# Attention of the last three batches computed token-major, with the square sums from ScalarE's accumulator

## The chip, the cores and the metric

The kernel runs on one core of a Trainium2 chip. The metric is the device time of one execution in microseconds (us). A core has TensorE (matrix products, PE), VectorE (DVE), ScalarE (ACT), GpSimd (POOL, which here issues most loads) and SyncE (SP, which here issues stores and transposing DMAs). Each engine works through its own queue in order; semaphores join the queues.

## What is computed

```python
def _attn_ref(q, k, v, g_norm):                   # q, k, v: [8 batches, 8 heads, 576 tokens, 64]
    kv = np.einsum('bhsd,bhse->bhde', k, v)
    out = np.einsum('bhsd,bhde->bhse', q, kv)
    rms = np.sqrt(np.mean(out * out, axis=-1, keepdims=True) + 1e-06)
    return (out / rms * g_norm).astype(np.float32)

def _moe_ref(x, w_a, w_b, w_out):                 # x: [4608, 512], w_a, w_b: [512, 1536]
    a = x @ w_a
    b = x @ w_b
    return (a * b @ w_out).astype(np.float32)
```

The attention's result is laid out as x, one row for a token and 8 heads of 64 columns, and goes through the bilinear layer. So each token's 64 values of a head are divided by their root mean square and multiplied by `g_norm`.

## The kernel before

**Stages.** The 4,608 tokens are cut into nine blocks of 512. For each block the layer's first half multiplies x with w_a and w_b, combines the two results and gives `ab`; the second half multiplies `ab` with w_out one block later, so that the two halves are interleaved in TensorE's queue. All blocks but the first use a fast scheme with seven products in place of eight (`wino_block`, `o_block`): sums of blocks of x are made first (`t_op`, L711), the products (L742) accumulate in banks of PSUM, ScalarE copies what stands in a bank between two products of a chain (L415), and VectorE adds such a copy to another bank (L761) and multiplies the two halves (L796). The second half's products are L911, ScalarE's copies from them L943, VectorE's sums L949, its sums of `ab` L896, and the stores L814.

**Attention.** Batches 0 and 1 are loaded in another layout at the start. Batches 2 to 7 go through `load_node` and `late_batch`. For a batch, GpSimd issues a copy of q to a DRAM scratch `scr` (L566) and the loads of k and v (L572 to L582); SyncE issues one transposing DMA that brings q from the scratch to the tile `qT`, with d on the partitions (L587). A one-element copy on GpSimd (`gate_t`, L563) holds the next batch's load back until the transpose of the batch before has landed. TensorE then makes k times v for all heads (L533, 20 products of 128 columns) and ScalarE copies it to a block-diagonal tile `kvd` that holds two heads (L548, L549).

`slices` does the rest, in eight slices a batch: four pairs of heads times two halves of 288 tokens. In each slice x stands d-major, with 2 x 64 values of d on the partitions and tokens along the columns. So a sum over d runs over partitions, and TensorE makes it with a matrix of ones:

```python
n1: PE   x_mm   L348   kvd x qT           -> PSUM, 288 columns
n2: ACT  sq_op  L358   Square             -> sq, 128 x 288
n3: PE   s_mm   L362   ones x sq          -> PSUM, 288 columns
n4: ACT  rs_op  L366   Abs_reciprocal_sqrt -> rs, 128 x 288
    DVE  xt_op  L371   x * g_col * rs     -> xp, d-major, as the layer reads it
```

The tiles `xp` hold x of four batches in a ring.

**The order.** No loop order decides what runs when. Every piece is a node of `Plan`, with an engine, a duration from a small formula (`mm_us`, `act_us`, `dve_us`), a priority time, what it depends on and what buffers it takes. `Plan.order` goes through the nodes by simulated time and writes one order for every engine; what the chip then does is this order, with real waits. `Buf` and `Ring` hand out buffers: attention has a pool of three PSUM banks (`PA`), of which `RQ` and `RS` use two each. `at_win[b]` is the window of time over which a batch's attention is spread by priority.

Of the kernel before, what the change touches and what calls it, by code (L numbers as in the profile page):

```python
# [8 lines left out]
FP32 = mybir.dt.float32  # L9
BF16 = mybir.dt.bfloat16  # L10
FP16 = mybir.dt.float16
AF = mybir.ActivationFunctionType
# [123 lines left out]
def kernel(  # L136
# [11 lines left out]
    nc = tc.nc  # L148

    B, H, S, D = q.shape  # L150
    d_model = H * D
# [4 lines left out]
    NP = H // 2  # L156
# [25 lines left out]
    EH = d_model // 2  # L182

    const = ctx.enter_context(tc.tile_pool(name="const", bufs=1))
    scr_pool = ctx.enter_context(tc.tile_pool(name="scr", bufs=B, space=bass.MemoryType.DRAM))
    psum = ctx.enter_context(tc.tile_pool(name="psum", bufs=1, space=bass.MemoryType.PSUM))
    ctx.enter_context(tc.manual_schedule())

    def sb(name, shape, dt):
        return const.tile(shape, dt, name=name)  # L190
# [15 lines left out]
    as_t = sb("as", [128, 4, NJ, 256], FP16)  # L206
    b_ts = [sb(f"c{i}", [128, 4, 2, NMAX], FP16) for i in range(2)]
    u_t = sb("u", [128, 6, 2, NMAX], FP32)
    sq_ts = [sb(f"sq{i}", [128, HF], BF16) for i in range(3)]
    rs_ts = [sb(f"rs{i}", [128, HF], FP32) for i in range(3)]  # L210
    o_ts = [sb(f"o_sb{i}", [128, 4, d_model], FP32) for i in range(2)]

# [95 lines left out]
    def xcols(p, t0, n):  # L308
        return xp[p // 2][:, p % 2, t0 % R : t0 % R + n]
# [94 lines left out]
    def act_us(n, bias=False):  # L404
        return (0.155 if bias else 0.06) + n / 1200

    def dve_us(n):
        return (n + 65) / 960
# [7 lines left out]
        ]  # L416

    T0 = 20.0
    plan = Plan({"PE": 5.7, "DVE": 3.3, "ACT": 2.7, "SP": 5.0, "POOL": 22.5, "V": 0.0})
    PB, PA, PO = Pool(banks[0:4]), Pool(banks[5:8]), Pool(banks[4:5])  # L420
    RX, RY, RO = Ring(PB, 2), Ring(PB, 2), Ring(PO)
    RQ, RS = Ring(PA, 2), Ring(PA, 2)
    RU, RB, RAB = Ring([u_t[:, i] for i in range(6)]), Ring(b_ts), Ring(ab_ts)
    RT, RAS = Ring([T_t[:, i] for i in range(5)]), Ring([as_t[:, i] for i in range(4)])
    RSQ, RRS, ROS = Ring(sq_ts), Ring(rs_ts), Ring(o_ts)
    RK, RV, RQT, RKD = Ring(k_ts), Ring(v_ts), Ring(qT_ts), Ring(kvd)
    normed = {}
# [14 lines left out]
    def slices(at, win, extra):  # L442
        w0, w1 = win
        for i in range(2 * NP):
            p, h = divmod(i, 2)
            pr = w0 + (w1 - w0) * i / (2 * NP)
            x, s = ((Buf(RX), Buf(RY)) if at.b == 0 and i % 3 == 1 else (Buf(RQ), Buf(RS)))
            sq, rs = Buf(RSQ), Buf(RRS)
            ta = at.b * S + h * HF
            war = [  # L450
                n
                for j, (a, b) in enumerate(blocks_of)
                if a < ta - R + HF and b > ta - R
                for n in readers.get(j, ())
            ]
            n1 = plan.add(
                "PE", mm_us(1, HF), pr,
                lambda p=p, h=h, x=x: at.x_mm(p, h, x.tile), extra(p), [x], at.qt,
            )
            n2 = plan.add(  # L460
                "ACT", act_us(HF), pr, lambda p=p, h=h, b=sq: at.sq_op(p, h, b.tile), [n1], [sq]
            )
            n3 = plan.add(
                "PE", mm_us(1, HF), pr,
                lambda p=p, h=h, s=s: at.s_mm(p, h, s.tile), [n2], [s], [sq],
            )
            s_done[at.b] = n3
            n4 = plan.add(
                "ACT", act_us(HF, True), pr,
                lambda p=p, h=h, b=rs: at.rs_op(p, h, b.tile), [n3], [rs], [s],  # L470
            )
            normed[at.b, p, h] = plan.add(
                "DVE", dve_us(HF) + 0.06, pr,
                lambda p=p, h=h: at.xt_op(p, h), [n4] + war + ([g_n] if at.b == 0 else []), (), [x, rs],
            )

    def early_batch(b, win):
# [35 lines left out]
            done[p] = [n2, n4]  # L513
        slices(at, win, lambda p: done[p])

    def late_batch(b, load, win):
        at = Attn(b)
        w0, w1 = win
        kb, vb, qb = load["k"], load["v"], load["q"]
        kd = Buf(RKD)  # L520
        at.qt = [qb, kd]

        def view(t):
            return t[:, 0 : H * (NCH + 1) * D].rearrange("p (h c d) -> p h c d", h=H, d=D)

        s = Buf(RS)

        def kv_mm():
            kv_ps = s.tile[:].rearrange("p (a e) -> p a e", a=NP)
            for c in range(NCH + 1):  # L530
                for p in range(NP):
                    hs = slice(2 * p, 2 * p + 2)
                    nc.tensor.matmul(  # L533
                        kv_ps[:, p, :],
                        lhsT=kb.tile[:, c, hs, :],
                        rhs=view(vb.tile)[:, hs, c, :],
                        start=(c == 0 and p == 0),
                        stop=(c == NCH and p == NP - 1),
                    )

        n = plan.add(
            "PE", 1.15, w0, kv_mm, [(load["n"], load["kv_us"]), plan.at(w0 - 3)], [s, kd], [kb, vb]
        )

        def kv_out():
            kv_ps = s.tile[:].rearrange("p (a e) -> p a e", a=NP)
            at.kvd = kd.tile
            nc.scalar.copy(at.kvd[0:D, :, 0:D], kv_ps[0:D, :, 0:D])  # L548
            nc.scalar.copy(at.kvd[D:, :, D:], kv_ps[D:, :, D:])  # L549
            for p in range(NP):  # L550
                at.q[p] = qb.tile[:, p, :]

        m = plan.add("ACT", 0.75, w0, kv_out, [n], (), [s])
        slices(at, (w0 + 0.12 * (w1 - w0), w1), lambda p: [m, (load["qn"], 8.0)])


    def load_node(b, prio, dep):
        ld = {"k": Buf(RK), "v": Buf(RV), "q": Buf(RQT)}
        scr = scr_pool.tile([NP, S, 2, D], BF16, name="scr", tag="scr")

        def issue():
            if dep is not None:
                nc.gpsimd.tensor_copy(gate_t, dep["q"].tile[0:1, 0, 0:1])  # L563
            qv = q[b].rearrange("(p hl) s d -> hl s p d", hl=2)
            for hl in range(2):
                nc.gpsimd.dma_start(  # L566
                    out=scr[:, :, hl, :].rearrange("p s d -> s p d"), in_=qv[hl]
                )
            kt = ld["k"].tile
            ks = k[b, :, 0:SA, :].rearrange("h (sp c) d -> sp h c d", c=NCH)  # L570
            for c in range(NCH):
                nc.gpsimd.dma_start(out=kt[:, c], in_=ks[:, :, c, :])  # L572
            nc.gpsimd.dma_start(out=kt[0:SB, NCH], in_=k[b, :, SA:S, :].rearrange("h sp d -> sp h d"))
            for n, src in (("v", v),):
                t = ld[n].tile[:, 0 : H * (NCH + 1) * D].rearrange(
                    "p (h c d) -> p h c d", h=H, d=D
                )
                nc.gpsimd.dma_start(
                    out=t[:, :, 0:NCH, :],
                    in_=src[b, :, 0:SA, :].rearrange("h (sp c) d -> sp h c d", c=NCH),  # L580
                )
                nc.gpsimd.dma_start(  # L582
                    out=t[0:SB, :, NCH, :], in_=src[b, :, SA:S, :].rearrange("h sp d -> sp h d")
                )

        def transpose():
            nc.sync.dma_start_transpose(  # L587
                out=ld["q"].tile[:].rearrange("p a s -> p (a s)"),
                in_=scr[:].rearrange("a s h d -> (a s) (h d)"),
            )  # L590

        issue_us, q_us, ld["kv_us"] = (15.4, 4.3, 13.0) if dep is None else (9.0, 5.0 if b == 3 else 1.8, 13.0)

        ld["n"] = plan.add(
            "POOL", issue_us, prio, issue, [(dep["qn"], 8.0)] if dep else [], [ld["k"], ld["v"]]
        )
        ld["qn"] = plan.add(
            "SP", 2.5, prio, transpose, [(ld["n"], q_us)], [ld["q"]]
        )
        return ld  # L600
# [422 lines left out]
    for b in range(2, B):  # L1023
        t = b * S / N0
        at_win[b] = (max(53.0, st[int(t) - 1] + (t % 1) * L[int(t) - 1] - 18), st[int(t)] - 22 + (t % 1) * 12)
    loads = {2: load_node(2, 22.5, None)}
    wo_n = load_wo(loads[2])
    for b in range(3, B):
        loads[b] = load_node(b, at_win[b - 1][0], loads[b - 1])
    gb = Buf(RQ)  # L1030
    g_in = plan.add(
        "PE", 0.07, 8.5, lambda: nc.tensor.transpose(gb.tile[:, 0:1], g_row, one), [plan.at(6.4)], [gb]
# [10 lines left out]
    for bi in range(1, nb + 1):  # L1043
        o_win = (st[bi] + 1.0, st[bi + 1] - 1.0) if bi < nb else (st[bi] + O_A, st[bi + 1] + O_B)
        if bi == 1:
            o_std(ab, muls, (o_win[0] + 4.0, o_win[1] + 4.0))
            osum = out_sums(st[2] - 10)
        else:
            o_block(bi - 1, ab, muls, osum, o_win, 2, (RO, RY, RY), 1)
        for b in needs[bi]:  # L1050
            late_batch(b, loads[b], at_win[b])
        ab, muls = wino_block(bi, (st[bi], st[bi + 1]), wsum)
    o_block(
        nb, ab, muls, osum, (st[nb + 1], st[nb + 1] + o_us[nb]), NJ // 2,
# [38 lines left out]
```

## Time and profile before

| | |
|---|---|
| time, median of 3 runs | 299.74 us (299.61 to 299.81) |
| the profiled execution | 299.53 us |
| its span in the profile | 297.8 us |
| busy: PE, DVE, ACT | 290.5, 234.0, 192.4 us |
| the chain of waits, by engine | PE 71%, DMA 22%, POOL 4% |
| squares L358, roots L366, multiplies L371 | 64 each, 414, 508 and 511 ns |
| k times v (L533), first and last | 51.2 and 206.5 us |
| transposes of q (L587), first and last | 42.2 and 155.5 us |

The span is what the profile covers of the execution; the rest of its time lies around it. A group's row gives line, engine, operation, the tiles and shapes, the count, then busy time and mean length of one, then the time that the engine stood idle just before and what ended it. The chain of waits is followed back from the end of the execution: it is carried by DMA while the weights and first batches arrive, and from 79.5 us on by TensorE's products.

### The profile page before, as it was taken

What the parts mean: (1) busy time and instruction counts of PE and PEld (TensorE: products, weight loads), DVE (VectorE), ACT (ScalarE), POOL (GpSimd) and SP (SyncE); (2) the same over time, 40 slices, a digit from 0 to 9 for tenths busy, and PEclk for the clock granted to TensorE, in tenths of its full rate; (3) what the DMA queues carried; (4) which work ended last, traced back from release to release, by engine and by line L of the source; (5) the groups of instructions that cost most, each with busy time, mean ns of one, the idle gap of its engine ahead of it and who ended that gap; (6) DMA issues with size and microseconds to landing.
All of it is one profiled execution on the core that took longest, in us unless ns stands there. A gap on an engine that the chain in (4) does not pass through costs nothing.

```text
span 297.8 us, 6705 instructions
## 1 busy us (share of the span) xinstructions
PE 290.5 (98%) x2635; PEld 238.9 (80%) x2635; DVE 234.0 (79%) x435; ACT 192.4 (65%) x401; POOL 76.7 (26%) x95
## 2 busy tenths in 40 slices
PE   8999999999899999999999999999999999999993
PEld 3645559865788988889888988889888888888882
DVE  5544879894976998889779977997599859897762
ACT  3847767865588577866787658954996466654521
POOL 8945830940190650380560000000000000000000
PEclk9999999999999999999999999999999999999999
DMA  8999999799999699699999200020004001100043
GB/s 178 199 199 199 194 159 155 119 166 186 202 113 172 94 191 174 42 136 210 136 146 222 74 0 2 36 108 0 2 0 143 1 2 70 73 3 0 34 144 108
DMA packets 98195, 32.72 MB, mean 110 GB/s; under 512 B 74612, under 2 KB 94068, under 8 KB 98164
## 3 DMA queue, kind: packets, MB, share of 16 engines
q0 software_dynamic: 77552, 18.44, 65.3%
q1 hardware_dynamic: 20000, 13.16, 20.3%
q10 hardware_dynamic: 612, 0.71, 0.8%
q8 instruction: 20, 0.33, 0.5%
q14 instruction: 11, 0.09, 0.1%
HBM read 37.75 MB, written 12.98 MB: 170 GB/s over the span
## 4 chain that ended last, share of the span: by engine, by line
PE 71%; DMA 22%; POOL 4%; issue 1%; DVE 1%; ACT 0%; DVEq 0%; SPq 0%; POOLq 0%
PE bk L742 42%; PE bk L911 24%; DMA scr<-in_q_dram 8%; DMA v_t<-in_v_dram 4%; DMA wb_t<-in_moe_w_b_dram 4%; DMA qT<-scr 3%; DMA wa_t<-in_moe_w_a_dram 3%; PE bk L362 2%; PE bk L348 2%; PE bk L533 2%; POOL as L237 1%; POOL so L237 1%; POOL scr L566 1%; DVE o_sb L949 1%; POOL wo_t L609 1%
## 5 line engine op out<-in xcount | busy, mean ns | idle before, releaser
L761 DVE TENSOR_TENSOR c<-bk,u 128x512 f16<-128x512 f32 x144 | 96.6, 685 | 25.2 <-ACT u L415 12.8
L415 ACT COPY u<-bk 128x512 f32<-128x512 f32 x144 | 81.8, 590 | 37.3 <-PE bk L742 33.8
L742 PE MATMUL bk<-xp,wa_t 128*128 128x256 f16 x288 | 54.9, 273 | 0.0
L742 PE MATMUL bk<-xp,wb_t 128*128 128x256 f16 x288 | 54.9, 273 | 0.0
L371 DVE SCALAR_TENSOR_TENSOR xp<-bk,g_col,rs 128x288 f16<-128x288 f32 x64 | 32.4, 511 | 14.3 <-ACT rs L366 14.3
L742 PEld LDWEIGHTS <-wa_t 128*128 128x128 f16 x384 | 37.4, 98 | 5.7
L911 PEld LDWEIGHTS <-abt 128*128 128x128 f16 x384 | 37.4, 98 | 4.7 <-DVE abt L796 0.2
L742 PEld LDWEIGHTS <-wb_t 128*128 128x128 f16 x384 | 37.6, 98 | 4.4
L415 ACT CAST c<-bk 128x512 f16<-128x512 f32 x48 | 28.1, 590 | 17.7 <-PE bk L742 16.9
L911 PE MATMUL bk<-wo_t,abt 128*128 128x256 f16 x288 | 36.8, 273 | 0.0
L742 PE MATMUL bk<-T,sb 128*128 128x256 f16 x192 | 36.6, 273 | 0.0
L742 PE MATMUL bk<-T,sa 128*128 128x256 f16 x192 | 36.6, 273 | 0.0
L366 ACT ACTIVATE rs<-bk,eps_t 128x288 f32<-128x288 f32 x64 | 32.3, 508 | 5.7 <-PE bk L362 5.2
L796 DVE TENSOR_TENSOR abt<-c 128x1024 f16<-128x1024 f16 x48 | 32.9, 686 | 1.8
L742 PEld LDWEIGHTS <-sa 128*128 128x128 f16 x288 | 28.1, 98 | 3.8
L911 PEld LDWEIGHTS <-as 128*128 128x128 f16 x288 | 28.2, 98 | 3.5
L742 PEld LDWEIGHTS <-sb 128*128 128x128 f16 x288 | 28.2, 98 | 3.3
L943 ACT COPY o_sb<-bk 128x512 f32<-128x512 f32 x31 | 18.2, 587 | 15.2 <-PE bk L911 14.8
L358 ACT ACTIVATE sq<-bk 128x288 bf16<-128x288 f32 x64 | 25.5, 414 | 1.3 <-PE bk L348 0.6
L911 PE MATMUL bk<-so,as 128*128 128x256 f16 x192 | 25.5, 273 | 0.0
L572 POOL DMA_DIRECT2D k_t<-in_k_dram x24 | 21.2, 897 | 0.7 <-issue 0.5
L566 POOL DMA_DIRECT2D scr<-in_q_dram x12 | 19.6, 1637 | 2.6 <-issue 1.4
(99 smaller groups left out, 396.5 us busy)
## 6 DMA issues: line engine op xcount, KB each, us to landing
out_dram<-o_sb SPq DMA_DIRECT2D x20, 256.0 KB, 2.3
scr<-in_q_dram POOLq DMA_DIRECT2D x12, 288.0 KB, 8.2
k_t<-in_k_dram POOLq DMA_DIRECT2D x24, 128.0 KB, 8.8
v_t<-in_v_dram POOLq DMA_DIRECT2D x6, 512.0 KB, 10.9
out_dram<-o_sb SPq DMA_DIRECT2D x18, 128.0 KB, 2.4
wa_t<-in_moe_w_a_dram POOLq DMA_DIRECT2D x6, 256.0 KB, 10.7
wb_t<-in_moe_w_b_dram POOLq DMA_DIRECT2D x6, 256.0 KB, 10.9
wo_t<-in_moe_w_out_dram POOLq DMA_DIRECT2D x2, 768.0 KB, 9.4
```

What stands on the lines that cost most here:

```text
L237: nc.gpsimd.dma_start(out=t[n][:, hs, :, :], in_=src[b, hs].rearrange("h (sp c) d -> sp h c d", c=EC),)
L358: nc.scalar.activation(sq, self.x_ps[p, h][:, 0:HF], AF.Square)
L366: nc.scalar.activation(rs, self.s_ps[p, h][:, 0:HF], AF.Abs_reciprocal_sqrt, bias=eps_t)
L371: nc.vector.scalar_tensor_tensor(out=xcols(p, self.b * S + h * HF, HF), in0=self.x_ps[p, h][:, 0:HF], scalar=g_col, in1=self.rs[p, h], op0 ...
L415: ("ACT", act_us(n), lambda: nc.scalar.copy(*args())),
L566: nc.gpsimd.dma_start(out=scr[:, :, hl, :].rearrange("p s d -> s p d"), in_=qv[hl])
L572: nc.gpsimd.dma_start(out=kt[:, c], in_=ks[:, :, c, :])
L742: nc.tensor.matmul(ps.tile[:, i * n : (i + 1) * n], lhsT=lhs(w, sm)[:, kc, :], rhs=rhs()[:, kc, :], start=start and i == 0 and kc == 0, st ...
L761: lambda: nc.vector.tensor_add(cs(fi, h), full(ps), u.tile),
L796: nc.vector.tensor_mul(t, c[:, :, :, 0], c[:, :, :, 1])
L911: nc.tensor.matmul(ps.tile[:, sub * EH : (sub + 1) * EH], lhsT=lhs(slice(j, j + 1))[:, 0, sub * 128 : (sub + 1) * 128], rhs=rhs[:, j, :], ...
L943: lambda: nc.scalar.copy(o(fi, h), bank(X, every)), [dep], takes, frees,
```

## The change

Batches 5, 6 and 7 (`TB = 5`) no longer go through `slices`. The new function `token_tiles` takes 128 tokens at a time, with tokens on the partitions and all 8 heads along 512 columns. A batch of 576 tokens has five such tiles; the fifth begins at token 448, so that its first half repeats 64 tokens, and only its last 64 rows are stored.

For a tile, TensorE makes four products with q as the stationary side and `kvd` as the moving side, 128 columns each, into one bank. A head's 64 values now lie along the columns of one partition, so ScalarE squares each head by itself and adds up its squares in its accumulator: eight instructions a tile, with a planned duration `SQ_US` of 0.113 us each. One root over 8 columns follows, then one multiply of 512 columns on VectorE, which gives x in 16 bits, token-major (`xt`). SyncE stores it to a DRAM scratch `xs`. When the batch's five tiles are stored, four transposing DMAs on SyncE bring x to `xp`, d-major, and VectorE multiplies it by g in place, in two instructions.

Around it: the windows of batches 5 to 7 are put 13 us earlier (`AHEAD`); the load of batch 7 is additionally held by a one-element copy that reads the turned x of batch 5 (the argument `xt` of `load_node`); loads are planned inside the loop over blocks; the planned arrival of batch 3's k and v is 16 us after the issue instead of 13; and there are two square buffers of 512 columns in place of three of 288, for all batches.

The order that the planner writes changes with this. Among the products of L742 and L911, k times v of batches 3 to 7 stood behind 192, 392, 688, 952 and 1,244 of them, and now stands behind 212, 396, 580, 868 and 1,152. The tiles of batches 5, 6 and 7 stand behind 592 to 676, 880 to 944 and 1,164 to 1,218. In SyncE's queue the transpose of batch 6's q comes between the stores of batch 5's first and second tile, and that of batch 7's q between those of batch 6's first and second tile.

```diff
-    sq_ts = [sb(f"sq{i}", [128, HF], BF16) for i in range(3)]
+    sq_ts = [sb(f"sq{i}", [128, d_model], BF16) for i in range(2)]
+    ss_t = sb("ss", [128, 3, 2 * H], FP32)
+    xt_t = sb("xt", [128, 2, d_model], FP16)
...
+    SQ_US = 0.113
+    TB, TURN, AHEAD = 5, 9.0, 13.0
...
+    def token_tiles(at, win, dep):
...
+        stored, tiles = [], [(i * 128, 128) for i in range(NCH)] + [(S - 128, SB)]
+        for i, (j0, keep) in enumerate(tiles):
...
+            X, sq, ss, xt = Buf(RQ), Buf(RSQ), Buf(RSS), Buf(RXT)
+
+            def mm(j0=j0, X=X):
+                for p in range(NP):
+                    nc.tensor.matmul(
+                        X.tile[:, p * 128 : (p + 1) * 128],
+                        lhsT=at.q[p][:, j0 : j0 + 128],
+                        rhs=at.kvd[:, p, :],
...
+            for h in range(H):
+                sl = slice(h * D, (h + 1) * D)
+                n3.append(
+                    plan.add(
+                        "ACT", SQ_US, pr,
+                        lambda X=X, sq=sq, ss=ss, sl=sl, h=h: nc.scalar.activation(
+                            sq.tile[:, sl], X.tile[:, sl], AF.Square, accum_out=ss.tile[:, h : h + 1]
+                        ),
...
+                lambda ss=ss: nc.scalar.activation(
+                    ss.tile[:, H:], ss.tile[:, 0:H], AF.Abs_reciprocal_sqrt, bias=eps_t, scale=1.0 / D
+                ),
...
+                lambda X=X, ss=ss, xt=xt, heads=heads: nc.vector.tensor_mul(
+                    heads(xt.tile), heads(X.tile[:]), ss.tile[:, H:].unsqueeze(2).to_broadcast([128, H, D])
+                ),
...
+            def save(j0=j0, keep=keep, xt=xt):
+                nc.sync.dma_start(
+                    out=xs[:, j0 + 128 - keep : j0 + 128, :].rearrange("a s e -> s a e"),
+                    in_=xt.tile[128 - keep :].rearrange("p (a e) -> p a e", a=NP),
+                )
...
+        def turn():
+            for p in range(NP):
+                nc.sync.dma_start_transpose(out=xcols(p, b * S, S), in_=xs[p])
+
+        n6 = plan.add("SP", 2.5, w1, turn, stored + war)
...
+                "DVE", 0.4, w1, lambda xg=xg: nc.vector.tensor_scalar_mul(xg, xg, g_col), [(n6, TURN)]
...
+        if b >= TB:
+            return token_tiles(at, (w0 + 0.12 * (w1 - w0), w1), [m, (load["qn"], 8.0)])
...
+            if xt is not None:
+                nc.gpsimd.tensor_copy(gate_t, xcols(NP - 1, (b - 2) * S, 1)[0:1])
...
-        issue_us, q_us, ld["kv_us"] = (15.4, 4.3, 13.0) if dep is None else (9.0, 5.0 if b == 3 else 1.8, 13.0)
+        issue_us, q_us, ld["kv_us"] = (15.4, 4.3, 13.0) if dep is None else (9.0, 5.0 if b == 3 else 1.8, 16.0 if b == 3 else 13.0)
...
+        if b >= TB:
+            at_win[b] = tuple(x - AHEAD for x in at_win[b])
...
-    for b in range(3, B):
-        loads[b] = load_node(b, at_win[b - 1][0], loads[b - 1])
...
-            late_batch(b, loads[b], at_win[b])
+            if b > 2:
+                loads[b] = load_node(b, at_win[b - 1][0], loads[b - 1], turned.get(b - 2))
+            turned[b] = late_batch(b, loads[b], at_win[b])
```

## The prediction

> **What bounds the kernel now.** I read the page first: its busy shares and slices.
>
> ```profile
> PE 290.5 (98%) x2635; PEld 238.9 (80%) x2635; DVE 234.0 (79%) x435; ACT 192.4 (65%) x401; POOL 76.7 (26%) x95
> PE   8999999999899999999999999999999999999993
> ACT  3847767865588577866787658954996466654521
> ```
>
> TensorE is busy in every slice but the last, so a microsecond taken from its queue is a microsecond gained, and one in which it waits is lost for good. ScalarE's 65% is a mean over stages. So next the busy time in stretches of 5 us where batches 6 and 7 are normalised (columns: stretch, length, then busy us with instruction counts of PE, weight loads, DVE, ACT, POOL; clock, DMA share, GB/s):
>
> ```profile
> 176.00:181.00 5.00, 5.00 (x48) 4.44 (x46) 2.60 (x6) 4.31 (x11) 0.00 (x0) 1.00 0.00 0
> 186.00:191.00 5.00, 5.00 (x47) 4.38 (x46) 4.97 (x11) 4.79 (x12) 0.00 (x0) 1.00 0.00 0
> 211.00:216.00 5.00, 5.00 (x48) 4.44 (x46) 2.99 (x6) 4.45 (x11) 0.00 (x0) 1.00 0.00 0
> 231.00:236.00 5.00, 5.00 (x48) 4.48 (x47) 5.00 (x11) 2.35 (x4) 0.00 (x0) 1.00 0.01 2
> ```
>
> ScalarE works 4.3 to 4.8 of 5 us while a batch's slices are under way, and 2.35 after them. What fills it, from the groups, and the waits (us in total, times, longest):
>
> ```profile
> L415 ACT COPY u<-bk 128x512 f32<-128x512 f32 x144 | 81.8, 590 | 37.3 <-PE bk L742 33.8
> L366 ACT ACTIVATE rs<-bk,eps_t 128x288 f32<-128x288 f32 x64 | 32.3, 508 | 5.7 <-PE bk L362 5.2
> L358 ACT ACTIVATE sq<-bk 128x288 bf16<-128x288 f32 x64 | 25.5, 414 | 1.3 <-PE bk L348 0.6
> ACT u L415 <- PE bk L742: 33.8, 59, 1.6
> PE bk L533 <- DMA v_t<-in_v_dram: 1.2, 1, 1.2
> ```
>
> The copies of L415 stand in the same queue as squares and roots, and TensorE needs them: the next product of a chain accumulates in the bank that the copy has just read. ScalarE arrives at most 1.6 us early for one; that is all the lateness TensorE can be spared. The last line is a stall of TensorE for batch 3's v.
>
> The paces, from the chain of waits (start, length, what), the timeline of ScalarE and the line of the q transposes:
>
> ```profile
> 205.62 1.12 PE bk L533 x20
> 253.26 10.48 PE bk L742 x96
> 7.73 0.21 ACT L329 CAST kvd<-bk 64x64 bf16<-64x64 f32 x1 [1.77 <-PE bk L320]
> 7.95 0.21 ACT L330 CAST kvd<-bk 64x64 bf16<-64x64 f32 x1
> 195.66 1.07 ACT L415 COPY u<-bk 128x512 f32<-128x512 f32 x2 [0.99 <-PE bk L742]
> L587 SPq DMA_TRANSPOSE qT<-scr x6: 5503/6154/6463, 42.2 to 155.5; - x6
> DMA to landing us min/median/max: 7.5/9.9/11.9
> 133.61 6.39 SPq L587 DMA_TRANSPOSE qT<-scr  x1
> ```
>
> A product of 256 columns takes 0.109 us of TensorE (10.48/96), one of 128 columns 0.056 (1.12/20), so one of 288 columns 0.123. Two 512-wide copies take 1.07 us, so one follows another after 0.48 us: 0.427 for its columns and 0.06. But two 64-wide casts out of one bank follow each other after 0.22 us, with nothing overlapped. A transpose of q holds SP's queue for about 6.2 us.
>
> **What the Trainium skill says.** "ScalarE: Activation LUTs", section "What ACT_TABLE_LOAD costs", gives an ACTIVATE 186 ns plus 0.833 ns an element, 93 ns more for a pointer operand, and an overlap of 93 ns back to back. The trace agrees on durations (414 ns against 426 for the square, 508 against 519 for the root). For 64 columns it would mean one every 146 ns; the nearest pair here took 0.22 us, and I let the trace decide. The same page says that ACTIVATE can give an accumulator output, without a price. "VectorE: DVE Perf Modes", section "Two Vector instructions with no wait between them", says that on VectorE an accumulator output is a second instruction. It is the same in this program: the built kernel has 120 additional ScalarE instructions, one behind each of its 120 squares. No run here shows one.
>
> **The change part by part.**
>
> TensorE. Three batches lose 8 slices with two products of 288 columns: 48 x 0.123 = 5.9 us. They gain 5 tiles of 4 products of 128 columns: 60 x 0.056 = 3.4 us. **Gain 2.5 us**, since it is TensorE's own path. Batch 3's k-v product moves 20 products (2.2 us) later in the queue, which should remove its 1.2 us wait (bounds 0 and 1.2; I take 1.2). Together **-3.7 us**.
>
> ScalarE. Per tile there are 8 squares of 64 columns with their 8 reads, and a root of 8 columns. Square: 0.22 us from the cast pair; low 0.113 (0.053 for 64 columns and the 0.06). Read: 0 if hidden, 0.20 if it costs a whole smallest instruction (the 0.21 us cast); I take 0.06, the gap between overlapping neighbours. The root is 508 - 240 + 7 = 0.275 us, and it waits until the last read is written: about 0.15 (the part of a cast's 0.21 us that isn't its columns); the low case takes 0.2 for both, since it overlaps. So a tile costs T = 8 x 0.28 + 0.43 = **2.65 us**; low 1.1; high 8 x 0.42 + 0.43 = 3.8. In the queue order, from the first to the last tile of batches 5, 6 and 7, 11, 7 and 8 copies stand between the squares: 5.3, 3.4 and 3.9 us at 0.48. TensorE has 84, 64 and 54 products between the first and last tile's, about 8 more until it needs the next copy, and 20 short ones: 11.2, 9.0 and 7.9 us. ScalarE needs 5T plus copies:
>
> - batch 5: 13.25 + 5.3 - 11.2 = 7.4 us more than TensorE
> - batch 6: 13.25 + 3.4 - 9.0 = 7.7
> - batch 7: 13.25 + 3.9 - 7.9 = 9.3
>
> That is 24.3 us. About 1.4 us a batch is free, since ScalarE now comes that early: 24.3 - 4.2 = **20.1 us of new TensorE stalls**. Low: nothing. High: 41.5 - 4.2 = 37.3. Behind a late square on ScalarE's queue stand L415's copies; VectorE's sums (L761) wait for these, and TensorE for both.
>
> VectorE. It loses 24 multiplies of 511 ns (12.3 us) and gets 15 of 512 columns from PSUM, as L761 does (685 ns, 10.3 us), and 6 scalings by g over 1,152 16-bit columns. No such row exists. The VectorE page's section "The perf-mode tier table" allows 4 columns a cycle for such an operation; by its figures I estimate 0.46 us, 1.4 if one column a cycle. That is +0.7 us (up to +6) over some 90 us in which VectorE has a tenth free: I take nothing. The cover is that gap; without it the whole sum would count.
>
> DMA and SP. Each batch gets five 64 to 128 KB stores (stores of that size land in 2.3 us here) and four transposes, together of q's size: some 6.2 us of SP and 9.9 to land. From the last tile to the block that reads its x, TensorE has 248, 232 and 210 products, 23 to 27 us. The chain is 4 us to the last store, 2.3 to land it, 10 for the turn, 1 for g and 2 for the block's first sums: 19 us, so hidden with 4 us over. Output stores queue behind the turns, but their buffers are wanted again only a block (some 30 us) later: nothing. POOL's load of batch 7 now waits for batch 5's turn, so it moves from 145 us to about 165; its k-v product is due after 197: nothing. The first batches get two square buffers for three; a square is read 0.3 us after it is made, and the next comes 0.4 later: nothing, bounds -0.5 and +0.5.
>
> Sum: -3.7 + 20.1 = +16.4 us on the profiled execution's own 299.53 us (span 297.8 and 1.7 around it), which lies 0.2 below the median of the three runs, 299.74. That gives **316 us**.
>
> **The rivals.**
>
> *The accumulator is nearly free* (chance 0.09). Squares overlap as the 512-wide copies do and the reads vanish: T = 1.1. Then the three excesses are -0.4, -0.1 and 1.5 us, within the free lateness but for 0.1, and -3.7 remains: 295.8 us, faster. For it: the 0.06 us between wide copies, and squares of different banks that overlap too. Against: the pair of 64-wide casts, and 120 instructions that must be executed. It decides at T = 1.56: then 12.6 + 15T - 28.1 is 7.9, which pays for 4.2 and 3.7. That is 0.14 us a head.
>
> *SP's queue becomes the wait* (0.14). Batch 6's q transpose stands between the stores of batch 5's first and second tile; it waits for its scratch until 133.6 and holds SP to 140. Tile 2's store leaves then and lands at 142.3; tile 4 needs that buffer, on VectorE, from about 137.5. That is 4 to 5 us there, and some 3.5 again in batch 6: 8 less 2 of slack, less 3.7, gives +2 to +3: 302 us. For it: the 6.39 us row. Against: if ScalarE is as slow as I think, tile 4 isn't ready before 143 anyway.
>
> *ScalarE bound* (0.77), as forecast: between T = 1.7 and 3.8, 302 to 333 us.
>
> **How the numbers follow.** A measurement of this kernel can tell 0.2%, 0.6 us. Faster 0.09 is the free accumulator; 0.03 for no change is where T falls at break-even, taken from the other two; 0.88 slower. The range goes from 300 (T = 1.6, just above break-even) to 333 (T = 3.8); the free case and a dearer read are left out.
>
> **What would show it.** In the profile after: squares of 64 columns with a second ScalarE row beside them, and one pair's pitch (0.28 us forecast, 0.14 the break-even); ScalarE near 5 of 5 us at the new places (about 128 to 150, 165 to 185 and 205 to 225 us); TensorE below 5 of 5 there and nowhere else, its waits named after ScalarE's copies or VectorE's sums; no wait of TensorE for v_t. If the gaps of TensorE end on stores of xt or on xs, SP was the reason; if x arrives late, T's sums (L711) would wait for the turn. A square with read under 0.14 us proves me wrong, and so do TensorE stalls outside the three windows.

## The result, and the profile after

The changed kernel takes 308.51 us (median of 4 runs, 308.15 to 309.09), the kernel before 299.68 us in the same session (299.61 to 299.81). The ratio is 1.0296, with a 95% interval from 1.0278 to 1.0314: **slower by 8.8 us**. The forecast was 316.0 us, with a range from 300 to 333 and 0.88 for slower. The profiled execution took 308.69 us, 9.2 us more than the one before (299.53), and its span is 306.9 us.

From the page of the changed kernel: busy shares, slices of the span, the chain by engine, and three groups.

```profile
PE 291.7 (95%) x2646; PEld 237.9 (78%) x2648; DVE 235.8 (77%) x432; ACT 201.1 (66%) x608; POOL 78.3 (25%) x96
PE   8999999999999999997899889998899999999993
ACT  3747667865688578799456995669756566564521
...
PE 76%; ACT 11%; DVE 5%; DMA 3%; POOL 2%; issue 1%; DVEq 0%; ACTq 0%; POOLq 0%
...
L418 ACT COPY u<-bk 128x512 f32<-128x512 f32 x144 | 84.4, 606 | 40.4 <-PE bk L832 37.2
...
L552 ACT ACTIVATE sq<-bk 128x64 bf16<-128x64 f32 x120 | 27.4, 321 | 0.0
L552 ACT ACTIVATION_READ_ACCUMULATOR sq<-bk 128x1 f32 x120 | 26.9, 306 | 0.0
```

TensorE's row of slices, 9 nearly everywhere before, now has six slices of 7 or 8 in three places. ScalarE's mean hardly moved (65% to 66%), but it now carries 11% of the chain that ends last; the page's shares by line give 6% to L552. Its two rows stand last above: 120 squares of 64 columns, and behind each a second instruction that reads the accumulator out. (Line numbers have moved: L742 is now L832, L911 is L1001, L415 is L418, L761 is L851, L587 is L677, L711 is L801.)

The busy time in stretches of 5 us, columns as in the prediction:

```profile
136.00:141.00 5.00, 4.09 (x38) 3.16 (x36) 3.77 (x8) 5.00 (x37) 0.00 (x0) 1.00 1.39 179
146.00:151.00 5.00, 3.61 (x33) 2.92 (x31) 4.34 (x8) 2.20 (x4) 0.00 (x0) 1.00 0.08 18
...
171.00:176.00 5.00, 3.81 (x32) 2.73 (x30) 4.44 (x8) 5.00 (x41) 0.00 (x0) 1.00 1.29 144
206.00:211.00 5.00, 3.77 (x37) 3.11 (x36) 3.66 (x7) 5.00 (x41) 0.00 (x0) 1.00 0.11 27
231.00:236.00 5.00, 5.00 (x49) 4.47 (x47) 5.00 (x12) 2.95 (x6) 0.00 (x0) 1.00 0.43 122
```

Where a batch's tiles stand, ScalarE (the fourth busy time) is at 5.00 of 5 us with some 40 instructions, and TensorE falls to 3.6 to 4.1. At 146 us ScalarE has already fallen to 2.20 and TensorE still lacks 1.4 us: that is the tail of a delay, handed on by VectorE (e3 below shows that it began with a store). After the last tile, TensorE is full again.

ScalarE's timeline at the first tile of batch 5 (start, length):

```profile
129.07 0.24 ACT L552 ACTIVATE sq<-bk 128x64 bf16<-128x64 f32 x1
129.19 0.21 ACT L552 ACTIVATION_READ_ACCUMULATOR sq<-bk 128x1 f32 x1
129.28 0.23 ACT L552 ACTIVATE sq<-bk 128x64 bf16<-128x64 f32 x1
129.38 0.22 ACT L552 ACTIVATION_READ_ACCUMULATOR sq<-bk 128x1 f32 x1
...
130.87 0.30 ACT L560 ACTIVATE ss<-ss,eps_t 128x8 f32<-128x8 f32 x1
131.07 0.57 ACT L418 COPY u<-bk 128x512 f32<-128x512 f32 x1
```

Read the starts, not the lengths: the lengths overlap. At the median of all tiles the read starts 0.104 us after its square, and the next square 0.093 after the read, so a head costs 0.197 us. From the first square to the copy behind the root this tile takes 131.07 - 129.07 = **2.0 us**, against 2.65 in the forecast.

The waits over the whole execution (us in total, times, longest):

```profile
DVE xt L567 <- ACT ss L560: 4.7, 7, 1.2
PE bk L832 <- ACT u L418: 4.0, 9, 0.9
PE bk L832 <- DVE c L851: 3.2, 7, 1.4
...
DVE xt L567 <- DMA xs<-xt: 1.8, 2, 1.4
```

TensorE waits for ScalarE's copies and for VectorE's sums, which themselves wait for ScalarE; both were named in advance. The wait for `v_t` is gone. The last row is the rival of SyncE's queue, small but there. The timeline of SP and of VectorE at that place:

```profile
132.53 6.91 SPq L677 DMA_TRANSPOSE qT<-scr  x1
140.64 0.40 SPq L574 DMA_DIRECT2D xs<-xt  x1
...
143.57 0.69 DVE L567 TENSOR_TENSOR xt<-bk,ss 128x512 f16<-128x512 f32 x1 [1.37 <-DMA xs<-xt]
```

The q transpose holds SP for 6.9 us, two output stores follow it, the second tile's store leaves only then, and the fourth tile's multiply, which needs that buffer, waits 1.37 us for it.

**The balance of TensorE.** Taking the products' starts one after another, and from each distance the product's own column time, what remains are TensorE's gaps. The distance from first to last product grew from 291.6 to 300.4 us, 8.8 us. The products' own time fell from 286.2 to 283.9 us, -2.3 (two records of 512 columns, 0.43 us together, are missing from the first 20 us of the changed kernel and of e1 to e4 below; they are filled in from a later run with the same products). The gaps grew from 5.4 to some 16.6 us, +11.2: 1.1 less in the first 90 us, where batch 3's wait went, and about 12 more at the tiles: 4.6 in batch 5, 3.3 in batch 6, 3.7 in batch 7, and 0.6 just before batch 6. These gaps are counted below in every kernel.

### The profile page after: what moved, and what is told of

It reads as the page before. It is cut to its first block, busy times and chain, and to the rows that moved or that the text cites. A ratio compares the mean times of both kernels' runs of the same rounds, so it can differ in the third digit from the quotient of the medians.

```text
span 306.9 us, 6973 instructions
## 1 busy us (share of the span) xinstructions
PE 291.7 (95%) x2646; PEld 237.9 (78%) x2648; DVE 235.8 (77%) x432; ACT 201.1 (66%) x608; POOL 78.3 (25%) x96
## 4 chain that ended last, share of the span: by engine, by line
PE 76%; ACT 11%; DVE 5%; DMA 3%; POOL 2%; issue 1%; DVEq 0%; ACTq 0%; POOLq 0%
PE bk L832 40%; PE bk L1001 21%; PE bk L385 7%; ACT sq L552 6%; PE bk L936 3%; DMA wb_t<-in_moe_w_b_dram 3%; ACT u L418 2%; PE bk L619 2%; PE bk L351 1%; PE bk L365 1%; DVE c L851 1%; POOL as L240 1%; ACT c L418 1%; ACT ss L560 1%; DVE xt L567 1%
## 5 line engine op out<-in xcount | busy, mean ns | idle before, releaser
L851 DVE TENSOR_TENSOR c<-bk,u 128x512 f16<-128x512 f32 x144 | 96.7, 686 | 28.3 <-ACT u L418 15.2
L418 ACT COPY u<-bk 128x512 f32<-128x512 f32 x144 | 84.4, 606 | 40.4 <-PE bk L832 37.2
L832 PE MATMUL bk<-xp,wa_t 128*128 128x256 f16 x288 | 54.9, 272 | 2.1 <-ACT c L418 1.2
L832 PE MATMUL bk<-xp,wb_t 128*128 128x256 f16 x288 | 55.0, 273 | 0.0
L832 PEld LDWEIGHTS <-wa_t 128*128 128x128 f16 x384 | 37.0, 98 | 9.8 <-issue 4.5
L1001 PEld LDWEIGHTS <-abt 128*128 128x128 f16 x384 | 37.4, 98 | 5.0 <-issue 0.5
L832 PEld LDWEIGHTS <-wb_t 128*128 128x128 f16 x384 | 37.5, 98 | 4.4
L418 ACT CAST c<-bk 128x512 f16<-128x512 f32 x48 | 28.5, 598 | 18.0 <-PE bk L832 17.2
L832 PE MATMUL bk<-T,sa 128*128 128x256 f16 x192 | 36.6, 272 | 3.3 <-ACT u L418 3.1
L1001 PE MATMUL bk<-wo_t,abt 128*128 128x256 f16 x288 | 37.1, 273 | 0.1
L832 PEld LDWEIGHTS <-sa 128*128 128x128 f16 x288 | 28.1, 98 | 11.1 <-issue 7.6
L832 PE MATMUL bk<-T,sb 128*128 128x256 f16 x192 | 36.6, 272 | 0.0
L1001 PEld LDWEIGHTS <-as 128*128 128x128 f16 x288 | 28.2, 98 | 3.3
L832 PEld LDWEIGHTS <-sb 128*128 128x128 f16 x288 | 28.1, 98 | 3.3
L374 DVE SCALAR_TENSOR_TENSOR xp<-bk,g_col,rs 128x288 f16<-128x288 f32 x40 | 20.3, 514 | 11.0 <-ACT rs L369 11.0
L552 ACT ACTIVATE sq<-bk 128x64 bf16<-128x64 f32 x120 | 27.4, 321 | 0.0
L552 ACT ACTIVATION_READ_ACCUMULATOR sq<-bk 128x1 f32 x120 | 26.9, 306 | 0.0
L1001 PE MATMUL bk<-so,as 128*128 128x256 f16 x192 | 25.7, 273 | 0.0
L369 ACT ACTIVATE rs<-bk,eps_t 128x288 f32<-128x288 f32 x40 | 20.0, 506 | 6.3 <-PE bk L365 6.1
## 6 DMA issues: line engine op xcount, KB each, us to landing
wb_t<-in_moe_w_b_dram POOLq DMA_DIRECT2D x6, 256.0 KB, 11.2
```

Source lines behind the costliest of these rows:

```text
L369: nc.scalar.activation(rs, self.s_ps[p, h][:, 0:HF], AF.Abs_reciprocal_sqrt, bias=eps_t)
L374: nc.vector.scalar_tensor_tensor(out=xcols(p, self.b * S + h * HF, HF), in0=self.x_ps[p, h][:, 0:HF], scalar=g_col, in1=self.rs[p, h], op0 ...
L418: ("ACT", act_us(n), lambda: nc.scalar.copy(*args())),
L552: lambda X=X, sq=sq, ss=ss, sl=sl, h=h: nc.scalar.activation(sq.tile[:, sl], X.tile[:, sl], AF.Square, accum_out=ss.tile[:, h : h + 1]),
L832: nc.tensor.matmul(ps.tile[:, i * n : (i + 1) * n], lhsT=lhs(w, sm)[:, kc, :], rhs=rhs()[:, kc, :], start=start and i == 0 and kc == 0, st ...
L851: lambda: nc.vector.tensor_add(cs(fi, h), full(ps), u.tile),
```

## The experiments

The kernel before took 299.56 to 299.66 us in these sessions, so medians can be set beside each other. Each kernel is the changed one with the edit shown, unless said otherwise.

### The read alone, the buffers alone, and both

e1 leaves out the sum over the squares, and so the read, with every order as it was.

```diff
+    nc.vector.memset(ss_t, 1.0)
-    sq.tile[:, sl], X.tile[:, sl], AF.Square, accum_out=ss.tile[:, h : h + 1]
+    sq.tile[:, sl], X.tile[:, sl], AF.Square
```

> The changed kernel with the squares left without an accumulator output, so that the 120 accumulator reads are not issued; the sums are a constant set once at the start, so the normalisation is left out. All orders are otherwise those of the changed kernel. ScalarE theory: the reads take 120 x 0.095 = 11.4 us of ScalarE, a tile then costs 8 x 0.105 + 0.4 = 1.24 us, below the 1.56 of the break-even, the stalls of TensorE at the tiles go to at most 2 us, and the time is 296.5 to 298.5 us. SP-queue theory: the tiles come earlier while the stores of xt leave as late as now, so VectorE waits longer for its buffers in batch 5 and the time stays at 300 us or above. TensorE theory (the short products cost more than 0.056 us): the time stays above 305 us.

Measured: 306.6 us (305.24 to 308.31), ratio 1.025. The ScalarE theory missed by 8 us and more. The four runs differ in TensorE's granted clock: 305.24 and 305.69 us came at 0.998 and 0.997, 307.51 and 308.31 at 0.984 and 0.989. So the edit alone is worth about 3 us at a full clock, and the median holds some of the fallen clock as well. TensorE's gaps fell only from 16.6 to 13.1 us, and what is left has another name. It is not that of the TensorE theory, though the time lies in its range: the short products start 0.056 us apart in the changed kernel too. From e1's waits, and after them one line of VectorE's timeline in e1:

```profile
DVE xt L568 <- DMA xs<-xt: 6.7, 3, 3.9
```

```profile
145.19 0.69 DVE L568 TENSOR_TENSOR xt<-bk,ss 128x512 f16<-128x512 f32 x1 [3.86 <-DMA xs<-xt]
```

In the changed kernel the same multiply started at 143.57 after waiting 1.37 us. Now ScalarE is ready early, and the multiply waits 3.86 us for the store behind the q transpose. Batches 5 and 6 kept 5.1 and 2.6 us of gaps, and the 0.7 before batch 6 stayed; batch 7, with no q transpose beside it, fell from 3.7 to 0.3. So ScalarE is what bounds batch 7, and in batches 5 and 6 a second wait stood ready behind it (in batch 6 the fourth multiply waits 1.84 us for a store).

e3 keeps the reads, and gives each of a batch's five tiles its own buffer, so that no multiply waits for the store of an earlier tile of its batch; orders are as they were.

```diff
-    xt_t = sb("xt", [128, 2, d_model], FP16)
+    xt_t = sb("xt", [128, 2 + NCH + 1, d_model], FP16)
-    ... heads(xt.tile), ...            # multiply, and the store's source
+    ... heads(xt_t[:, 2 + i]), ...
```

> The changed kernel with a buffer of its own for each of a batch's five token-major tiles in place of two in turn, in the same orders on all engines. SP-queue theory: VectorE's 1.8 us of waits for the stores of xt in batch 5 go, and TensorE's last stall there (1.4 us) with them: 306.5 to 307.2 us. ScalarE theory: in that stretch VectorE and TensorE wait for ScalarE anyway, and the wait only changes its name: 308 to 308.5 us.

Measured: 307.28 us (306.88 to 307.54), ratio 1.0253 (1.0239 to 1.0267): 1.2 us less than the changed kernel. Batch 5's gaps fell from 4.6 to 2.9 us: the two at 148 and 149 us, 1.7 together, are gone. Batch 6 kept 3.3, batch 7 3.6, and the 0.6 before batch 6 stayed. So while the reads are there, SP is worth 1.2 us and only in batch 5.

f1 does both edits.

> The changed kernel without the 120 accumulator reads (sums set to a constant once, so the normalisation is left out) and with a buffer of its own for each of a batch's five token-major tiles, in the same orders. Two-wait theory: ScalarE's reads and the stores held up in SP's queue are the only two things that stop TensorE at the tiles, each hidden behind the other in part. With both gone the stalls of 12.2 us go and the time is 299.6 - 0.8 (early part) - 2.5 (TensorE's shorter work) = 296.3, within 295.8 to 297.3 us. If a third wait stands behind them (VectorE, the turned x, PSUM banks), the time is 299 us or more.

Measured: 299.83 us (298.71 to 301.58 in 12 runs), ratio 1.0007 (0.9991 to 1.0022), 3.5 us more than expected. Still, the square of four is clear:

| | two buffers | five buffers |
|---|---|---|
| squares with reads | 308.51 | 307.28 |
| squares without | 306.6 | 299.83 |

Each edit alone gives 1.9 (about 3 at a full clock) or 1.2 us; together 8.7. In batches 5 and 6 the two delays run side by side, and only the longer one shows. The profiled execution of f1 has 6.9 us of gaps, some 2.5 at the tiles, of which 0.8 follows the scaling by g of batch 5 (below). So there is a third wait, the rival in f1's expectation. Why f1's runs spread over 3 us was not found; their granted clock was 0.996 to 1.000 in all.

### Doubling the cost

e2 issues each square with its read twice, into the same sum.

```diff
-    lambda ...: nc.scalar.activation(..., AF.Square, accum_out=ss.tile[:, h : h + 1]),
+    lambda ...: [nc.scalar.activation(..., AF.Square, accum_out=ss.tile[:, h : h + 1])
+                 for _ in range(2)],
```

> The changed kernel with each of the 120 squares and its accumulator read issued twice, one behind the other; the result is the same. ScalarE theory: 120 x 0.197 = 23.6 us more of ScalarE inside the three stretches where it is already the bound, nearly all of it on TensorE's path: 308.5 + 22 to 24 = 330 to 333 us. SP-queue theory: the tiles only come later, the stores are waited for less, and at most 8 us are added: below 317 us.

Measured: 350.91 us (350.23 to 351.89), ratio 1.1713, some 18 us more than expected. ScalarE's timeline shows why:

```profile
128.99 0.24 ACT L553 ACTIVATE sq<-bk 128x64 bf16<-128x64 f32 x1
129.10 0.21 ACT L553 ACTIVATION_READ_ACCUMULATOR sq<-bk 128x1 f32 x1
129.34 0.22 ACT L553 ACTIVATE sq<-bk 128x64 bf16<-128x64 f32 x1
129.46 0.19 ACT L553 ACTIVATION_READ_ACCUMULATOR sq<-bk 128x1 f32 x1
129.56 0.22 ACT L553 ACTIVATE sq<-bk 128x64 bf16<-128x64 f32 x1
```

The repeat into the same sum (and the same columns of `sq`) starts 0.24 us after the read, not 0.093, as the read ends. The first head takes 129.56 - 128.99 = 0.57 us, the median one 0.55. The addition is 120 x (0.55 - 0.197) = 42 us, and the time grew by 42.4, so ScalarE's time at the tiles lies on the path. One thing blurs this: TensorE's granted clock also fell here, to 0.50 in the stretch from 151 to 156 us, which no theory had named. The slower pace of the products themselves comes to some 13 us; how much of that is hidden behind ScalarE was not separated.

### The planner's price

In the changed kernel the planner takes 0.113 us for a square, 0.197 was measured; an order written for cheap tiles packs them too closely. f3 sets the price to 0.2 and takes the five buffers; g2 sets the price alone.

```diff
-    SQ_US = 0.113
+    SQ_US = 0.2
```

> The changed kernel with five tile buffers, and with the planner told 0.2 us for a square with its read in place of 0.113; the orders are written anew. If only the planner's price is wrong, it places the copies ahead of the squares where TensorE needs them, and the time is 297 to 300 us. If ScalarE's capacity in windows this short is what lacks, it stays within 2 us of the run with five buffers: 305 to 308 us.

> The changed kernel with the planned duration of a square and its read at 0.2 us, near the measured 0.197, and nothing else changed: two buffers of xt as in the changed kernel. Theory (the planner's price spreads the squares, which took 6.5 us off the kernel with five buffers; the two buffers leave the third tile's multiply of batch 5 waiting for a store behind the q transpose): 301.5 to 303.5 us, with a wait of VectorE on a store of 1 to 4 us. Rival (once the tiles are planned wider apart, two buffers are enough): 300.5 to 301.3 us, as with five.

Measured: f3 300.79 us (300.53 to 301.36), ratio 1.0044 (1.003 to 1.0059), 0.8 above the upper end that the planner theory gave and far below the other; g2 305.43 us (303.91 to 306.12), ratio 1.0187 (1.016 to 1.0215), 2 us above the dearer of its two expectations. Two of g2's four runs, 303.91 and 304.8 us, had a granted clock of 0.999; the other two, at 0.986 and 0.993, took 306.1.

| | two buffers | five buffers |
|---|---|---|
| price 0.113 | 308.51 | 307.28 |
| price 0.2 | 305.43 | 300.79 |

The price takes 6.5 us off with five buffers and 3.1 with two (some 4 at a full clock). ScalarE does the same work in f3; it only has more work of TensorE beside it. From the first to the last tile of batches 5, 6 and 7 stand 88, 88 and 76 of TensorE's 256-column products in f3's order, against 84, 64 and 54 in the changed kernel's. Two stretches of 5 us of f3:

```profile
136.00:141.00 5.00, 4.74 (x43) 3.75 (x42) 4.61 (x9) 5.00 (x38) 0.00 (x0) 1.00 1.43 143
...
206.00:211.00 5.00, 5.00 (x50) 4.51 (x49) 5.00 (x9) 5.00 (x36) 0.00 (x0) 1.00 0.12 30
```

ScalarE is again at 5.00, with nearly the same count, but TensorE is at 4.74 and 5.00, where the changed kernel had 4.09 and 3.77. f3 keeps 3.7 us of gaps at the tiles, 1.5 of them in batch 7 between 201 and 205 us, and 0.7 before batch 6. A full engine is not yet a wait; it depends on what stands between two things that need it.

Why g2 missed, in the timeline of SP and of VectorE:

```profile
109.43 28.60 SPq L677 DMA_TRANSPOSE qT<-scr  x2
138.13 0.52 SPq L574 DMA_DIRECT2D xs<-xt  x1
...
141.69 0.69 DVE L567 TENSOR_TENSOR xt<-bk,ss 128x512 f16<-128x512 f32 x1 [2.70 <-DMA xs<-xt]
```

The new order puts batch 6's q transpose ahead of the first store instead of the second, and now the third tile waits for its buffer, 2.70 us. Of g2's 14.0 us of gaps 6.3 are there. In the stretch from 141 to 146 us the granted clock fell to 0.61, so that some 3 us of these gaps are slow products, not waiting.

### The early part of the change

e4 takes no tiles at all (`TB = 8`) and keeps the rest: the later planned arrival of batch 3's k and v and the two square buffers among it. f4 is the kernel before with that arrival alone.

```diff
-    TB, TURN, AHEAD = 5, 9.0, 13.0                                  # e4
+    TB, TURN, AHEAD = 8, 9.0, 13.0
-    (9.0, 5.0 if b == 3 else 1.8, 13.0)                             # f4, in the kernel before
+    (9.0, 5.0 if b == 3 else 1.8, 16.0 if b == 3 else 13.0)
```

> Everything of the change but the token-major tiles themselves: all batches d-major (TB = 8), with the two square buffers, the loads planned inside the loop over blocks, and batch 3's planned arrival of 16 us. No batch's window is moved, as that goes with the tiles. If the early part is worth what TensorE's gaps show (1.1 us less at batch 3, 0.5 us more before 40 us), the time is 298.8 to 299.4 us. If two square buffers cost the first batches more than that, it is above 299.8.

> The kernel before with one number changed: the planned arrival of batch 3's k and v is 16 us after their issue in place of 13, nothing else. If the early part's gain is this number, 298.6 to 299.0 us, as without the tiles; if it comes from the other edits, 299.4 us or more.

Measured: e4 298.80 us (298.29 to 298.90), ratio 0.9968 (0.9956 to 0.9981), gaps 4.6; f4 298.31 us (298.16 to 298.50), ratio 0.9961 (0.9947 to 0.9975), gaps 4.0. The single number 16 is worth 1.25 us, as TensorE's wait of 1.2 for `v_t` said. e4 lies 0.5 above f4, in gaps before 20 us; what makes them was not tried. The 0.5 us more before 40 us that e4's expectation reckons with was not there: it was the two missing records of the changed kernel, whose gaps before 40 us are, with them, those of the kernel before. The tiles therefore cost 308.51 - 298.80 = 9.7 us.

### Tiles without the accumulator

f2 squares a tile in one instruction of 512 columns on ScalarE and lets VectorE add up the heads, with five buffers. g1 does this for batch 7 alone (`TB = 7`), which meets neither a q transpose nor a load. h1 and h2 are g1 and f2 with the scalings by g moved to ScalarE.

```diff
-    for h in range(H): ... nc.scalar.activation(sq.tile[:, sl], X.tile[:, sl], AF.Square, accum_out=...)
+    nc.scalar.activation(sq.tile, X.tile[:], AF.Square)
+    nc.vector.tensor_reduce(ss.tile[:, 0:H], heads(sq.tile), axis=mybir.AxisListType.X, op=ALU.add)
-    "DVE", 0.4, w1, lambda xg=xg: nc.vector.tensor_scalar_mul(xg, xg, g_col)         # h1, h2
+    "ACT", act_us(1152, True), w1, lambda xg=xg: nc.scalar.mul(xg, xg, g_col)
```

> The changed kernel with five tile buffers, and with one square of 512 columns on ScalarE and one sum over each head's 64 columns on VectorE in place of the eight squares with accumulators; the planner knows the new pieces and writes its orders anew. ScalarE theory: a tile takes 0.48 + 0.4 us of ScalarE instead of 2.0, VectorE gets 15 x 0.6 = 9 us more, which its idle tenth can hold only in part: 296.5 to 299.5 us. Rival: VectorE, busy 4.5 of 5 us there, becomes the wait: 301 us or more.

> Only batch 7 is token-major, with one 512-wide square on ScalarE, its sums by head on VectorE, and a buffer for each tile; batches 5 and 6 go as before. Theory (what is left of the loss stands where the q transposes and GpSimd's load issue meet the tiles, in batches 5 and 6; batch 7 has neither): a third of TensorE's saving (0.8 us) comes through whole on top of the 298.31 us of the kernel before with the later k and v of batch 3, so 297.3 to 298.0 us. Rival (the tiles themselves cost as much as they save, wherever they stand): 298.3 us or more.

> As g1 (batch 7 alone token-major, square 512 wide on ScalarE, sums by head on VectorE, own buffers), with the two scalings by g moved from VectorE to ScalarE, which the planner prices at 1.115 us each. Theory (in g1 VectorE is busy without a gap around its two g scalings and T's sums, and TensorE waits for it twice, 1.05 us; without the scalings both waits go): 297.8 to 298.4 us, and no gap of TensorE over 0.2 us where batch 7 is turned. Rival (any other engine's delay there takes the place, or the tiles cost by themselves): 298.9 us or more.

> As f2 (batches 5 to 7 token-major, square 512 wide on ScalarE, sums by head on VectorE, own buffers), with the six scalings by g moved to ScalarE. Theory (f2 keeps about 2 us of gaps at the tiles, the largest, 0.71 us, behind the scaling of batch 5, which took VectorE 1.96 us beside GpSimd's load issue): without it on VectorE 296.8 to 297.8 us. Rival (the scaling isn't what delays TensorE): 298.2 us or more.

| kernel | us | ratio (interval) | TensorE's products, gaps |
|---|---|---|---|
| f4 (no tiles) | 298.31 | 0.9961 (0.9947 to 0.9975) | 286.2, 4.0 |
| f2 (three batches) | 298.41 | 0.9966 (0.9954 to 0.9979) | 283.9, 6.6 |
| h2 (three, g on ScalarE) | 298.54 | 0.9963 (0.995 to 0.9975) | 283.9, 6.3 |
| g1 (one batch) | 299.29 | 0.9988 (0.9981 to 0.9994) | 285.6, 5.4 |
| h1 (one, g on ScalarE) | 298.35 | 0.9958 (0.9946 to 0.9971) | 285.6, 5.4 |

f2 is 10 us faster than the changed kernel with the same products on TensorE: the per-head squares and reads, their price, and the two buffers together are the loss. But no kernel with tiles is faster than f4. The theory for g1 missed (299.29, where 297.3 to 298.0 was expected). The timeline of TensorE and of VectorE in g1, where batch 7's x is scaled:

```profile
228.02 0.38 PE L834 MATMUL bk<-xp,wa_t 128*128 128x256 f16 x2 [0.40 <-DVE c L853]
...
229.82 0.38 PE L834 MATMUL bk<-xp,sa 128*128 128x256 f16 x2 [0.33 <-DVE c L853]
...
223.62 0.94 DVE L597 TENSOR_SCALAR xp<-xp,g_col 128x1152 f16<-128x1152 f16 x2
```

The busy time there, in stretches of 5 us of g1:

```profile
218.00:223.00 5.00, 5.00 (x49) 4.49 (x47) 4.32 (x8) 2.50 (x5) 0.00 (x0) 1.00 0.52 113
223.00:228.00 5.00, 4.62 (x43) 4.00 (x41) 5.00 (x12) 3.17 (x6) 0.00 (x0) 1.00 0.42 158
228.00:233.00 5.00, 4.65 (x42) 4.00 (x42) 5.00 (x11) 2.76 (x6) 0.00 (x0) 1.00 0.01 2
```

VectorE (the third busy time) is full from the scaling on, and TensorE loses 0.7 us, with two waits for VectorE's sums. In h1 and h2 the scaling is on ScalarE. Its row in the groups of h2 (busy us, mean ns of one, idle before):

```profile
L597 ACT ACTIVATE xp<-xp,g_col 128x1152 f16<-128x1152 f16 x6 | 7.2, 1254 | 0.0
```

For such an instruction the formula of the Trainium skill, "ScalarE: Activation LUTs", section "What ACT_TABLE_LOAD costs", gives 186 + 1,152 x 0.833 + 93 = 1,239 ns, an estimate with which the trace agrees.

h1's time fell into the expected range, by 0.9 us against g1, but its profiled execution has the same 5.4 us of gaps, in other places, 1.1 of them at the same block. So the waits didn't go, and the range was met by luck: from the first to the last product TensorE takes 290.95 us in g1 and 290.94 in h1, and what differs lies behind the last products. The end of the timeline of g1 and, behind the dots, of h1:

```profile
290.95 1.47 PE L1003 MATMUL bk<-wo_t,as 128*128 128x256 f16 x12
292.86 1.29 ACTq L906 DMA_DIRECT2D out_dram<-o_sb  x2
...
291.15 1.25 PE L1003 MATMUL bk<-so,abt 128*128 128x256 f16 x10
292.08 0.88 ACTq L906 DMA_DIRECT2D out_dram<-o_sb  x2
```

The planner, given the edit, also wrote another order for the last block: its last products are others, and the last stores leave 0.8 us earlier. In h2 the same move gave nothing: 298.54 against 298.41. Where TensorE's 2.3 us went with three batches is shown only as a sum: gaps of 6.3 to 6.6 against 4.0. The saving of TensorE is given back in small waits.

f4, h1, f2 and h2 lie 1.1 to 1.3 us below the kernel before and can't be told from each other; f4 does it with one number.

## Why the prediction was right in kind, and wrong in size

**The mechanism held.** ScalarE was to be the bound at the tiles, TensorE to wait there for copies and for sums behind them, and the result to be slower. The windows, the waits and the doubling show it. The measured +8.8 us is little more than half of the forecast +16.4, and two errors of opposite sign made it come that near: ScalarE's work was priced 12 us too high, and waits of SP and VectorE, priced at nothing, are in the measurement.

**TensorE, -3.7.** Forecast -2.5 and -1.2; the products' own time fell by 2.3, and the wait for `v_t` by 1.1, and f4, with the later arrival alone, gained 1.25 us. Both right.

**The mis-sized term: a square and its read, 8 x 0.28 us.** Measured: 8 x 0.197. The square was priced at 0.22 us from two casts of 64 columns that didn't overlap; it overlaps and takes 0.104, under even the low bound of 0.113. The formula of the Trainium skill ("ScalarE: Activation LUTs", section "What ACT_TABLE_LOAD costs") gives 0.146 us as an estimate; the measured pitch is lower still. The read was taken at 0.06 and takes 0.093. So the first tile takes 2.0 us and not 2.65 (the forecast's own terms give 2.67). Most tiles take less, for the root's wait for the last read is covered. ScalarE's timeline at the third tile of batch 5:

```profile
138.02 0.27 ACT L552 ACTIVATION_READ_ACCUMULATOR sq<-bk 128x1 f32 x1
138.12 0.36 ACT L560 ACTIVATE ss<-ss,eps_t 128x8 f32<-128x8 f32 x1
138.33 0.27 ACT L552 ACTIVATE sq<-bk 128x64 bf16<-128x64 f32 x1
```

Here the fourth tile's first square and read stand between, and the root starts 0.10 us after a read and holds the queue for 0.21. In 11 of the 15 tiles a copy or such a square covers the wait, and T is 8 x 0.197 + 0.21 = 1.8 us; the mean of all is 1.85. That takes 15 x 0.80 = 12 us off the sum: 316 becomes 304. The measured 0.197 us a head lies above the break-even of 0.14, but the break-even itself is not confirmed: f1, at 0.104 a head and with SP's wait gone, should by the sum have come to 296.3 us and took 299.83.

**The sum with the measured T.** The same windows and the same 1.4 us of free lateness give 9.25 + 5.3 - 11.2 - 1.4 = 1.95 us for batch 5, 2.25 for batch 6 and 3.85 for batch 7; measured were 4.6, 3.3 and 3.7. In batch 5 SP has its part: with five buffers its gaps are 2.9. So of the 4.5 us between 304 and the measurement, SP has some 1.7, the gap before batch 6 has 0.6, and about 2 us in batches 5 and 6 are assigned by no run. Reading stalls from the queue order, copies and products between the first and last tile, worked to about a microsecond a batch once SP was out.

**SP as a rival.** Its mechanism and place were right: the store left at 140.64, where 140 was forecast. Wrong was to set it beside ScalarE as an alternative. Both hold at once, and the later one shows. "Tile 4 isn't ready before 143 anyway" was wrong by 1.4 us, about what e3 gave back. Tile 4's root ended at 141.57:

```profile
141.13 0.44 ACT L560 ACTIVATE ss<-ss,eps_t 128x8 f32<-128x8 f32 x1
```

**VectorE at nothing.** The scaling was estimated at 0.46 us an instruction; four of the six took about 0.5 us, the two of batch 5 some 0.7 and 0.97. The cover, "a tenth free over 90 us", was a mean: where the scaling falls, VectorE is full. In the changed kernel 0.6 us of gaps follows it before batch 6, just outside the windows in which alone the prediction allowed stalls: one of its own signs of being wrong, and true by that much. In g1 two waits follow it.

**Hidden as forecast:** x comes in time, with no wait of T's sums for the turn; the load of batch 7 moves to 156 us (165 forecast), and no wait of TensorE names it, though the slow scalings of batch 5 stand beside its issue; the changed kernel's gaps in the first batches are those of the kernel before, with two square buffers for three.

## What to carry to other kernels

Price a small instruction by the distance of starts between neighbours, not by its recorded length or by a look-alike, and count what it issues besides itself. When one wait is removed, look for the one that stands ready behind it before any gain is promised: two edits were worth 1.9 and 1.2 us alone and 8.7 together. In a planned order a wrong duration is a cost by itself: 0.113 for 0.197 us was worth 3 to 6.5 us here, with not one instruction changed.

## What was not expected of the hardware

- A ScalarE accumulator output is a separate instruction, recorded with 306 ns on average, but 0.093 us from its start to the next square. A square into the same sum and columns starts 0.24 us after it.
- TensorE's granted clock fell at long stalls: to 0.50 in a stretch of e2, at one of 3.4 us, and to 0.61 in one of g2, at one of 2.8 us. In the profiled execution of e1 a stall of 2.8 us left it at full, as did those of up to 1.5 us in the changed kernel. What decides was not tested.
- The 16-bit scaling of 1,152 columns took 0.51 us, and 0.97 where GpSimd was issuing the load of batch 7 beside it; in f2 the pair of batch 5 took 1.96 us against 0.94 for the others. The slow ones all stood beside that issue, but not all beside it were slow: in f1 the second of the pair took 0.50. What decides was not tried.
- A transpose of a quarter of x holds SP for some 1.26 us, and lands after 2.7; one of a whole q holds it for 4.1 to 6.9 us in the changed kernel, and landed after some 9.9 at the median of both kernels.
